# Weight conversion spread over the score units, masks moved to GpSimd, and products two blocks later, in a routed-attention and ELU kernel

## The chip, the cores and the metric

The kernel runs on one core of a Trainium2 chip. The metric is the device time of one execution in microseconds. Three runs of the kernel before took 1084.14, 1084.19 and 1082.23 us (median 1084.14). Its profile is of another execution, which took 1081.5 us with a span of 1078.2 us. The engines are called PE (matmuls; PEld is its weight load), DVE (VectorE), ACT (ScalarE), POOL (GpSimd) and SP (which issues the DMAs).

## The reference

Four batches of eight heads, 768 tokens of 64 elements each. Every query and key is assigned to one of 16 centroids of its head; attention is allowed only where the two assignments agree. Its output, as 3072 tokens of 512, goes through an MLP with an ELU.

```python
mask = q_assign[:, :, :, None] == k_assign[:, :, None, :]
scores = scale * np.matmul(q, k.transpose(0, 1, 3, 2))
scores = np.where(mask, scores, -1000000000.0)
...
attn = np.exp(scores)
attn = attn / (np.sum(attn, axis=-1, keepdims=True) + 1e-09)
...
h = x @ w_in                       # 512 x 2048
g = np.where(h > 0.0, h, alpha * (np.exp(np.minimum(h, 0.0)) - 1.0))
return (g @ w_out).astype(np.float32)   # 2048 x 512
```

Both weights arrive as 64-bit floats, everything else as 32-bit.

## The kernel before, in words

**Blocks.** Attention is done in 48 blocks: four batches, three thirds of the queries (256 tokens), four pairs of heads. In a block, `scores(n)` has three units. A unit is 128x1024 scores in one PSUM buffer of two banks (matmuls L398 for q times k, L407 for the mask), which ACT turns into `p` with an exponential (L415). `values(n)` multiplies `p` with v into `o_bank` (L442) and sums the rows into a buffer `d` with a matrix of ones (L431): 24 matmul records from `p` itself or, where `sums(n)` has added the three units on DVE first (L419 to L421), only 4. ACT copies `o_bank` to `xT` (L456) and `d` to `r` (L458), DVE takes the reciprocal (L459), POOL multiplies (L460). `check(n)` reads `r` again on ACT for a running sum (L466). The units, `d` and the hidden matmuls share three PSUM buffers (`banks`).

**Masks.** `assign` makes one-hot assignments `hot` on DVE (L349 to L364) from similarities that PE computes (L332). `masks(n)` turns those of the queries into 0 or minus 2^80 (L375: m times x minus m, two instructions on ACT, 64x256 bf16 each) for the matmul L407 of block n.

**MLP.** After four blocks a third of the tokens is complete. Its MLP has four groups of work, one for each later block: hidden 0 and 1; hidden 2 and 3; products 1 to 4; products 5 to 7. `hidden` runs 32 matmuls (64 records, L481, for two of them), an exponential on ACT (L491), a clamp on POOL (L492) and `elu` on DVE (L498 to L502), which is issued one `hidden` late, from a list called `lag`. The product with `w_out` is done with seven half-size block products instead of eight (L511), in the manner of Strassen and Winograd: g is cut in four (a_, b_, c_, d_), `w_out` in four (e_, f_, g_, h_), and sums of the cuts are made once for the weights (`sum_weights`, on POOL and DVE, L296 to L299) and per third for g. The products alternate between the PSUM banks `o_bank` and `f_bank`.

**Weights.** The 64-bit weights are loaded as 32 pieces of 128x512 (16 of `w_in`, 16 of `w_out`), as pairs of 32-bit words, into memory that is free at the time. `weight_steps` is a generator; each step issues, for one piece: on DVE the mantissa bits (L252) and the exponent bits into a tile `ex` (L255); one step later, on ACT the mantissa to a float, 2^-20 x + 1 (L247), and the exponent's new bias (L248); on DVE the sign (L258) and the low word (L261); on POOL the final product (L264). `weigh(k)` takes k steps. It is called four times a step in blocks 0 to 3 and five after each step of the MLP in blocks 4 and 5; in block 6 what is left and `sum_weights` come before the first products.

**Order.** The order of work on each engine is that of the program's text. The main loop takes block n: `values(n-1)`, loads, `scores(n)`, `check(n-1)`, `masks(n+1)`, `sums(n)` from n = 6 on, then group n-4 of the MLP (`LAG = 4`). At the last block of a batch the next batch's routing (`similar`, `assign`) is spread between the steps of that group; with LAG at 4 this is the group of products 5 to 7.

Of the kernel before, what the change touches and what calls it, by code (L numbers as in the profile page):

```python
# [9 lines left out]
F32 = mybir.dt.float32  # L10
BF16 = mybir.dt.bfloat16
# [7 lines left out]
P = 128  # L19
# [41 lines left out]
def main_path(ctx, tc, c, q, k, v, centroids, moe_w_in, moe_w_out, out):  # L61
# [100 lines left out]
    for e in range(2):  # L162
# [4 lines left out]
            axis=Axis.XY,  # L167
            op=Alu.add,
        )
    minus = const.tile([P, 2], F32, name="minus")  # L170
    nc.vector.tensor_scalar(minus, big, -BIG, None, op0=Alu.mult)
    nc.vector.tensor_scalar(big, big, BIG, None, op0=Alu.mult)

    sq = const.tile([P, D], F32, name="sq")
# [37 lines left out]
    ]  # L212
    into = len(pieces)
    pieces += [(w_out[:, f], moe_w_out[ts(f, P)]) for f in range(FC)]
    one = const.tile([P, 1], F32, name="one")
    off = const.tile([P, 1], F32, name="off")
    nc.gpsimd.memset(one, 1.0)
    nc.gpsimd.memset(off, -896.0 * 2**23)
    words, exps = {}, {}
    places = []  # L220
# [19 lines left out]

    def weight_steps():

        for n in range(len(pieces) + 1) if wide else ():
            if n > 0:
                to = pieces[n - 1][0]
                ex = exps[n - 1]
                nc.scalar.activation(to, to.bitcast(U32), Act.Identity, scale=2.0**-20, bias=one)  # L247
                nc.scalar.activation(ex, ex, Act.Relu, scale=8.0, bias=off)  # L248
            if n < len(pieces):
                high = words[n][0][:, :, 1]  # L250
                e = exps[n] = loads.tile([P, WC], U32, name="ex", tag="ex", bufs=2)
                nc.vector.tensor_scalar(  # L252
                    pieces[n][0].bitcast(U32), high, 0xFFFFF, None, op0=Alu.bitwise_and
                )
                nc.vector.tensor_scalar(e, high, 0x7FF00000, None, op0=Alu.bitwise_and)  # L255
            if n > 0:
                w, place, limit = words.pop(n - 1)
                nc.vector.scalar_tensor_tensor(  # L258
                    ex, w[:, :, 1], 0x80000000, ex, op0=Alu.bitwise_and, op1=Alu.bitwise_or
                )  # L260
                nc.vector.scalar_tensor_tensor(  # L261
                    to, w[:, :, 0], 2.0**-52, to, op0=Alu.mult, op1=Alu.add
                )
                nc.gpsimd.tensor_tensor(to, to, ex.bitcast(F32), op=Alu.mult)  # L264
                places.append((place, limit))
                ask()
            yield
# [4 lines left out]
    places += [(spare[:, ts(n, 2 * WC)], into + 2 * n - 1) for n in range(FC * DM // (2 * WC))]  # L272
    ask()
    rest = weight_steps()

# [93 lines left out]
    def masks(n):  # L369
        b, third, pr = blocks[n]  # L370
        qm[n] = route.tile([P, QS], BF16, name="qm", tag="qm", bufs=2)
        for e in range(2):
            rows = slice(64 * e, 64 * e + 64)
            m = big[rows, pr % 2 : pr % 2 + 1]
            nc.scalar.activation(  # L375
                qm[n][rows],
                hot[b, 0][rows, side(pr, e), ts(third, QS)],
                Act.Identity,
                scale=m,
                bias=minus[rows, pr % 2 : pr % 2 + 1],  # L380
            )

# [5 lines left out]
    def scores(n):  # L388
        b, third, pr = blocks[n]
        i = b * NPR + pr  # L390
        cols = ts(third, QS)
        for u in range(NT // 2):
            s = banks()
            for m in range(2):
                kt = 2 * u + m
                for e in range(2):
                    rows = slice(64 * e, 64 * e + 64)
                    nc.tensor.matmul(  # L398
                        s[:, e, ts(m, QS)],
                        lhsT=T[i, 1][rows, ts(kt, P)],  # L400
                        rhs=T[i, 0][rows, cols],
                        start=True,
                        stop=False,
                    )
                for e in range(2):
                    rows = slice(64 * e, 64 * e + 64)
                    nc.tensor.matmul(  # L407
                        s[:, e, ts(m, QS)],
                        lhsT=hot[b, 1][rows, side(pr, e), ts(kt, P)],
                        rhs=qm[n][rows],  # L410
                        start=False,
                        stop=True,
                    )
# [48 lines left out]

    def check(n):

        seen_r = work.tile([P, QS], BF16, name="seen_r", tag="seen_r", bufs=1)
        nc.scalar.activation(seen_r, rs.pop(n), Act.Copy, accum_out=r_sum[:, n : n + 1])  # L466


    lag = []
# [36 lines left out]
                op=Alu.subtract,  # L506
            )

    def product(to, left, right, more=False):
        for f in range(FC // 2):  # L510
            nc.tensor.matmul(  # L511
                to[:, :QS],
                lhsT=left[:, f],
                rhs=right[:, f],
                start=(f == 0 and not more),
                stop=(f == FC // 2 - 1),
                skip_group_check=more,
            )

    def outer(b, third):  # L520
# [5 lines left out]
        seen = {}  # L526

        def temp():
            return loads.tile([P, 2, QS], F32, name="part", tag="ex", bufs=2)

        def out_tile():
            return work.tile([P, DM], F32, name="o_sb", tag="o_sb")
# [83 lines left out]
    for n in range(len(blocks) + LAG):  # L616
# [7 lines left out]
                load("k", (b + 1) * NPR + pr)  # L624
        if n + 1 < len(blocks):
            load_v(n + 1)
        if n < len(blocks):
            scores(n)
        if 0 < n <= len(blocks):
            check(n - 1)  # L630
        if n < len(blocks):
            if at + 1 < NB:
                masks(n + 1)
            if n >= LAG + 2:
                sums(n)
            if ahead and at in turns:
                for j in range(2):
                    turn((b + 1) * NPR + turns[at], j)
# [15 lines left out]
        for m, step in enumerate(main):  # L654
# [279 lines left out]
```

## Time and profile before

| what | from the profile | us |
|---|---|---|
| span | page | 1078.2 |
| PE busy, 27.7 to 161.5 us | busy time by stretch | 94.7 of 133.8 |
| PE busy, 188.5 to 1053 us | busy time by stretch | 863.4 of 864.5 |
| PE waiting for ACT's copy to `r` (L458) at L398 | waits | 27.4, six times |
| DVE waiting for ACT's exponent (L248) at L258 | waits | 24.2, six times |
| DVE's L255 waiting for POOL's product (L264) | waits | 13.9 + 12.8 |
| conversion on ACT: L247, L248 | groups | 23.0, 22.9 |
| conversion on POOL: L264 | groups | 22.1 + 21.7 |
| masks on ACT: L375 | groups | 56.8 (96 of 0.59) |
| clamp on POOL: L492, 1024 elements | groups | 1.06 each |

The page cuts the span in 40 slices of 27 us and gives the busy share of each engine in tenths; PEclk is the clock that PE was granted. A timeline line has start, duration, engine, line of the kernel, operation, output, inputs with shapes, and in brackets the idle time just before with what ended it. The span falls in two stages: to about 189 us PE is often idle while the weights are converted and summed; after that it is busy without a gap until the last products.

### The profile page before, as it was taken

How to read it: one execution, taken by the hardware profiler on the slowest of the kernel's cores; microseconds unless marked ns; L12 is line 12 of the kernel's file. 1: busy time of each engine (PE TensorE's matmuls, PEld its weight loads, DVE VectorE, ACT ScalarE, POOL GpSimd, SP SyncE). 2: the span in 40 equal slices, each digit the busy share in tenths (PEclk: the TensorE clock that was granted, in tenths of full speed). 3: DMA queues.
4: the chain of work that ended last, by engine and by line, in shares of the span. 5: the costliest groups of instructions: out<-in, count | busy, mean ns of one | idle time of the engine just before them, and what ended most of it. 6: DMA issues, size and time to landing. Idle time of an engine off the chain costs nothing.

```text
span 1078.2 us, 14856 instructions
## 1 busy us (share of the span) xinstructions
PE 1012.6 (94%) x6323; PEld 782.4 (73%) x6323; DVE 500.1 (46%) x624; ACT 381.9 (35%) x651; POOL 163.9 (15%) x164
## 2 busy tenths in 40 slices
PE   6778477999999999999999999999999999999996
PEld 4446355787688788787678788788678788788785
DVE  5565667444744334344744344344753344334231
ACT  4765451432333333432333333432243333432210
POOL 0333345110011111110011111110011111111110
PEclk9989688999999999999999999999999999999999
DMA  9734330131100230131100230131100100100000
GB/s 283 255 104 134 81 64 1 50 62 27 49 16 15 64 60 15 49 62 27 50 16 15 63 61 15 49 60 30 49 15 16 49 15 16 49 16 16 20 1 22
DMA packets 103960, 55.58 MB, mean 52 GB/s; under 512 B 83408, under 2 KB 96720, under 8 KB 103888
## 3 DMA queue, kind: packets, MB, share of 16 engines
q1 hardware_dynamic: 103888, 54.57, 18.8%
q8 instruction: 51, 0.84, 0.3%
q14 instruction: 21, 0.17, 0.0%
HBM read 48.27 MB, written 6.29 MB: 51 GB/s over the span
## 4 chain that ended last, share of the span: by engine, by line
PE 82%; DVE 9%; POOL 4%; issue 2%; ACT 2%; DMA 0%; POOLq 0%; ACTq 0%
PE banks L481 30%; PE f_bank L511 15%; PE o_bank L511 12%; PE banks L398 11%; PE o_bank L442 10%; PE banks L407 3%; PE banks L431 2%; POOL w_out L264 2%; POOL w_in L264 1%; DVE ex L258 1%; DVE oh L351 1%; PE banks L332 1%; DVE hot L361 1%; DVE ex L255 1%; DVE w_in L261 1%
## 5 line engine op out<-in xcount | busy, mean ns | idle before, releaser
L481 PE MATMUL banks<-xT,w_in 128*128 128x256 f32 x1536 | 338.4, 381 | 1.3 <-DVE gT L498 1.3
L481 PEld LDWEIGHTS banks<-xT,w_in 128*128 128x128 f32 x1536 | 290.5, 190 | 47.8 <-ACT p L415 3.2
L398 PE MATMUL banks<-qT,kT 64*128 64x256 f32 x1152 | 176.7, 404 | 38.1 <-ACT r L458 27.4
L415 ACT ACTIVATE p<-banks 128x1024 f32<-128x1024 f32 x144 | 147.0, 1025 | 46.8 <-PE banks L407 42.4
L459 DVE RECIPROCAL r<-r 128x256 f32<-128x256 f32 x48 | 84.0, 1750 | 161.8 <-ACT r L458 161.7
L398 PEld LDWEIGHTS banks<-qT,kT 64*128 64x128 f32 x1152 | 91.6, 195 | 90.2 <-ACT r L458 30.3
L442 PE MATMUL o_bank<-p,v_raw 128*64 128x256 f32 x1152 | 141.4, 386 | 0.0
L491 ACT ACTIVATE gT<-banks 128x1024 f32<-128x1024 f32 x48 | 49.1, 1023 | 240.9 <-PE banks L481 240.9
L498 DVE SCALAR_TENSOR_TENSOR gT<-gT,banks 128x1024 f32<-128x1024 f32 x48 | 58.4, 1216 | 163.0 <-POOL gT L492 163.0
L442 PEld LDWEIGHTS o_bank<-p,v_raw 128*64 128x64 f32 x1152 | 78.8, 137 | 51.7 <-issue 15.0
L492 POOL TENSOR_SCALAR gT<-gT 128x1024 f32<-128x1024 f32 x48 | 50.9, 1060 | 317.1 <-ACT gT L491 317.1
L511 PE MATMUL f_bank<-w_out,gT 128*128 128x256 f32 x384 | 89.8, 387 | 7.9 <-POOL w_out L297 7.9
L460 POOL TENSOR_TENSOR xT<-xT,r 128x256 f32<-128x256 f32 x48 | 38.6, 804 | 345.3 <-DVE r L459 345.3
L511 PE MATMUL o_bank<-w_out,gT 128*128 128x256 f32 x384 | 89.1, 386 | 0.0
L511 PEld LDWEIGHTS f_bank<-w_out,gT 128*128 128x128 f32 x384 | 73.8, 193 | 21.0 <-POOL w_out L297 9.0
L407 PE MATMUL banks<-qm,hot 64*128 64x256 bf16 x576 | 83.8, 277 | 2.8 <-DVE hot L361 2.8
L511 PEld LDWEIGHTS o_bank<-w_out,gT 128*128 128x128 f32 x384 | 73.1, 193 | 13.3 <-issue 3.5
L456 ACT COPY xT<-o_bank 128x256 f32<-128x256 f32 x48 | 17.8, 370 | 160.7 <-PE o_bank L442 160.7
L375 ACT ACTIVATE qm<-hot,minus,big 64x256 bf16<-64x256 bf16 x96 | 56.8, 591 | 35.4 <-DVE hot L361 34.2
L419 DVE TENSOR_TENSOR psum<-p 128x1024 f32<-128x1024 f32 x42 | 51.2, 1219 | 34.8 <-ACT p L415 34.8
L420 DVE TENSOR_TENSOR psum<-psum,p 128x1024 f32<-128x1024 f32 x42 | 52.8, 1257 | 4.9 <-ACT p L415 1.6
L511 PE MATMUL f_bank<-w_sum,g_sum 128*128 128x256 f32 x192 | 44.6, 386 | 0.5 <-ACT part L559 0.5
(110 smaller groups left out, 811.7 us busy)
## 6 DMA issues: line engine op xcount, KB each, us to landing
v_raw<-in_v_dram SPq DMA_DIRECT2D x48, 384.0 KB, 3.2
out_dram<-o_sb SPq DMA_DIRECT2D x24, 256.0 KB, 2.1
w_sum<-in_moe_w_out_dram SPq DMA_DIRECT2D x11, 512.0 KB, 3.7
q_raw<-in_q_dram SPq DMA_DIRECT2D x48, 96.0 KB, 3.9
k_raw<-in_k_dram SPq DMA_DIRECT2D x48, 96.0 KB, 3.4
w_sum<-in_moe_w_in_dram SPq DMA_DIRECT2D x8, 512.0 KB, 7.7
w_out<-in_moe_w_in_dram SPq DMA_DIRECT2D x8, 512.0 KB, 10.2
w_out<-in_moe_w_out_dram SPq DMA_DIRECT2D x5, 512.0 KB, 3.7
```

Of the source, the lines that this page charges most:

```text
L375: nc.scalar.activation(qm[n][rows], hot[b, 0][rows, side(pr, e), ts(third, QS)], Act.Identity, scale=m, bias=minus[rows, pr % 2 : pr % 2 + 1],
L398: nc.tensor.matmul(s[:, e, ts(m, QS)], lhsT=T[i, 1][rows, ts(kt, P)], rhs=T[i, 0][rows, cols], start=True, stop=False,)
L407: nc.tensor.matmul(s[:, e, ts(m, QS)], lhsT=hot[b, 1][rows, side(pr, e), ts(kt, P)], rhs=qm[n][rows], start=False, stop=True,)
L415: nc.scalar.activation(p, s, Act.Exp, scale=SCALE)
L419: nc.vector.tensor_tensor(to, pu[n, 0], pu[n, 1], op=Alu.add)
L420: nc.vector.tensor_tensor(to, to, pu[n, 2], op=Alu.add)
L442: nc.tensor.matmul(o_bank[64 * e : 64 * e + 64, :QS], lhsT=raw["v", n][:, e, kt], rhs=p[:, e, ts(m, QS)], start=(kt == 0), stop=(kt == NT ...
L459: nc.vector.reciprocal(r, r)
L481: nc.tensor.matmul(hf[:, f], lhsT=w_in[:, ch, ts(4 * n + f, P)], rhs=xT[b, third][:, ch], start=(ch == 0 and f % 2 == 0), stop=(ch == KC - 1),
L492: nc.gpsimd.tensor_scalar(t, t, 1.0, 0.0, op0=Alu.min, op1=Alu.max)
L498: nc.vector.scalar_tensor_tensor(t, t, -1.0, hf, op0=Alu.add, op1=Alu.max)
L511: nc.tensor.matmul(to[:, :QS], lhsT=left[:, f], rhs=right[:, f], start=(f == 0 and not more), stop=(f == FC // 2 - 1), skip_group_check=more,)
```

## The change

- `weight_steps` works over three pieces: in step k DVE does the two mantissa and exponent operations of piece k, ACT the exponent of piece k-1, and POOL the mantissa to float of piece k-1 (a `tensor_scalar` from uint32, which was ACT's L247), then DVE the sign and low word of piece k-2 and POOL the product of piece k-2. `ex` has three buffers instead of two.
- One step is issued after each of the three score units in blocks 0 to 7, and two after each step of the MLP in blocks 6 and 7. The four steps at the end of a block are gone.
- `LAG` is 6: each MLP group comes two blocks later, `sums` start at block 8, and the group beside the routing at a batch's end is now hidden 2 and 3.
- `masks` is a `tensor_scalar` on POOL, and is issued ahead of `scores(n)`. `minus` and `one` are gone.
- The second and third product change places and banks, and no product accumulates on another's bank; two ACT copies become DVE additions that read `f_bank`.
- `check` writes over `r`, and `sq` uses the buffer of `r`.

```diff
     def weight_steps():
-        for n in range(len(pieces) + 1) if wide else ():
-            if n > 0:
-                to = pieces[n - 1][0]
-                ex = exps[n - 1]
-                nc.scalar.activation(to, to.bitcast(U32), Act.Identity, scale=2.0**-20, bias=one)
-                nc.scalar.activation(ex, ex, Act.Relu, scale=8.0, bias=off)
+        for n in range(len(pieces) + 2) if wide else ():
             if n < len(pieces):
                 high = words[n][0][:, :, 1]
-                e = exps[n] = loads.tile([P, WC], U32, name="ex", tag="ex", bufs=2)
+                e = exps[n] = loads.tile([P, WC], U32, name="ex", tag="ex", bufs=3)
...
-            if n > 0:
-                w, place, limit = words.pop(n - 1)
+            if 0 <= n - 1 < len(pieces):
+                to, ex = pieces[n - 1][0], exps[n - 1]
+                nc.scalar.activation(ex, ex, Act.Relu, scale=8.0, bias=off)
+                nc.gpsimd.tensor_scalar(
+                    to, to.bitcast(U32), 2.0**-20, 1.0, op0=Alu.mult, op1=Alu.add
+                )
+            if n > 1:
+                to, ex = pieces[n - 2][0], exps.pop(n - 2)
+                w, place, limit = words.pop(n - 2)
...
-            nc.scalar.activation(
+            nc.gpsimd.tensor_scalar(
                 qm[n][rows],
                 hot[b, 0][rows, side(pr, e), ts(third, QS)],
-                Act.Identity,
-                scale=m,
-                bias=minus[rows, pr % 2 : pr % 2 + 1],
-            )
+                m,
+                m,
+                op0=Alu.mult,
+                op1=Alu.subtract,
+            )
+    LAG = 6
...
             nc.scalar.activation(p, s, Act.Exp, scale=SCALE)
+            if n < LAG + 2:
+                weigh(1)
...
-        seen_r = work.tile([P, QS], BF16, name="seen_r", tag="seen_r", bufs=1)
-        nc.scalar.activation(seen_r, rs.pop(n), Act.Copy, accum_out=r_sum[:, n : n + 1])
+        r = rs.pop(n)
+        nc.scalar.activation(r, r, Act.Copy, accum_out=r_sum[:, n : n + 1])
...
         def second():
-            product(f_bank, c_, f_)
-            nc.scalar.copy(seen["ae"][:, 1], f_bank[:, :QS])
+            product(f_bank, b_, g_)
+            o0, _ = seen["o"] = out_tile(), out_tile()
+            nc.vector.tensor_tensor(o0[:, :QS], f_bank[:, :QS], seen["ae"][:, 0], op=Alu.add)
+            nc.vector.tensor_tensor(b_, b_, g_sum, op=Alu.subtract)

         def third_():
-            product(o_bank, b_, g_, more=True)
-            seen["o"] = out_tile(), out_tile()
-            nc.scalar.copy(seen["o"][0][:, :QS], o_bank[:, :QS])
-            nc.vector.tensor_tensor(b_, b_, g_sum, op=Alu.subtract)
+            product(o_bank, c_, f_)
+            nc.scalar.copy(seen["ae"][:, 1], o_bank[:, :QS])

         def fourth():
-            product(f_bank, d_, t4, more=True)
+            product(f_bank, d_, t4)
             seen["dt"] = temp()
-            nc.scalar.copy(seen["dt"][:, 0], f_bank[:, :QS])
+            nc.vector.tensor_tensor(
+                seen["dt"][:, 0], f_bank[:, :QS], seen["ae"][:, 1], op=Alu.add
+            )
...
-    LAG = 4
...
+        if n + 1 < len(blocks) and at + 1 < NB:
+            masks(n + 1)
         if n < len(blocks):
             scores(n)
         if 0 < n <= len(blocks):
             check(n - 1)
         if n < len(blocks):
-            if at + 1 < NB:
-                masks(n + 1)
...
-        if n < LAG:
-            weigh(4)
...
             if n < LAG + 2:
-                weigh(5)
+                weigh(2)
```

The conversion's lines in the changed kernel are L244 and L247 (mantissa and exponent bits, DVE), L250 (exponent, ACT), L251 (mantissa to float, POOL), L257 and L260 (sign, low word, DVE) and L263 (product, POOL). L374 is the masks, L401 and L410 the score matmuls, L464 the reciprocal, L465 the `xT` product, L548 and L553 the first two DVE operations of the products.

More of the change, by code (lines that the diff above doesn't have):

```diff
@@ L169, in main_path @@
         )
-    minus = const.tile([P, 2], F32, name="minus")
-    nc.vector.tensor_scalar(minus, big, -BIG, None, op0=Alu.mult)
     nc.vector.tensor_scalar(big, big, BIG, None, op0=Alu.mult)
-    sq = const.tile([P, D], F32, name="sq")
+    sq = work.tile([P, D], F32, name="sq", tag="r", bufs=1)
     ss = const.tile([P, 1], F32, name="ss")
@@ L214, in main_path @@
     pieces += [(w_out[:, f], moe_w_out[ts(f, P)]) for f in range(FC)]
-    one = const.tile([P, 1], F32, name="one")
     off = const.tile([P, 1], F32, name="off")
-    nc.gpsimd.memset(one, 1.0)
     nc.gpsimd.memset(off, -896.0 * 2**23)
@@ L271, in main_path @@
     spare = w_out.rearrange("p f m -> p (f m)")
-    places += [(spare[:, ts(n, 2 * WC)], into + 2 * n - 1) for n in range(FC * DM // (2 * WC))]
+    places += [(spare[:, ts(n, 2 * WC)], into + 2 * n - 2) for n in range(FC * DM // (2 * WC))]
     ask()
@@ L507, in elu, with product @@
             )
-    def product(to, left, right, more=False):
+    def product(to, left, right):
         for f in range(FC // 2):
@@ L514, in product @@
                 rhs=right[:, f],
-                start=(f == 0 and not more),
+                start=(f == 0),
                 stop=(f == FC // 2 - 1),
-                skip_group_check=more,
             )
@@ L528, in temp @@
         def temp():
-            return loads.tile([P, 2, QS], F32, name="part", tag="ex", bufs=2)
+            return loads.tile([P, 2, QS], F32, name="part", tag="ex", bufs=3)
         def out_tile():
```

## The prediction

> **What bounds the kernel now.** I read the page's slices first: PE is at 9 tenths from the eighth slice (189 us) on and far below it before, so there are two stages.
>
> ```profile
> span 1078.2 us, 14856 instructions
> PE   6778477999999999999999999999999999999996
> DVE  5565667444744334344744344344753344334231
> POOL 0333345110011111110011111110011111111110
> PEclk9989688999999999999999999999999999999999
> ```
>
> Busy time by stretch says the same: PE is busy 863.4 of the 864.5 us from 188.5 on, but 94.7 of 133.8 between 27.7 and 161.5 us, where the 32 weight pieces are converted. Only two things can move the span: that first stage, and new holes in PE's later work. The timeline of DVE and of POOL shows what paces the conversion:
>
> ```profile
> 35.37 0.43 DVE L255 TENSOR_SCALAR ex<-w_sum 128x512 uint32<-128x512 uint32 x1 [1.16 <-POOL w_in L264]
> 35.72 0.68 DVE L258 SCALAR_TENSOR_TENSOR ex<-w_sum,ex 128x512 uint32<-128x512 uint32 x1
> 36.32 0.69 DVE L261 SCALAR_TENSOR_TENSOR w_in<-w_sum,w_in 128x512 f32<-128x512 uint32 x1
> 36.92 0.42 DVE L252 TENSOR_SCALAR w_in<-w_sum 128x512 uint32<-128x512 uint32 x1
> 37.08 1.39 POOL L264 TENSOR_TENSOR w_in<-w_in,ex 128x512 f32<-128x512 f32 x1 [1.74 <-DVE w_in L261]
> 38.50 0.43 DVE L255 TENSOR_SCALAR ex<-w_sum 128x512 uint32<-128x512 uint32 x1 [1.16 <-POOL w_in L264]
> ```
>
> One piece takes 38.50 - 35.37 = 3.13 us and is a closed ring: L255 waits until POOL's product L264 has freed the `ex` buffer, then L258, L261, and the next L264. Once per block a piece takes 6.0 us (L264 starts at 40.22, then at 46.22), since ACT waits for the reciprocal and does the masks (1.2 us) ahead of it. Four pieces and a block take 15.4 us (reciprocals at 40.05, 55.43, 70.82). The last L264 ends at 161.5, and two sum passes follow. The fourth product ends at 188.5, where the next values begin: that instant is my marker.
>
> The second thing to see is how DVE and POOL meet:
>
> ```profile
> 109.85 1.27 POOL L264 TENSOR_TENSOR w_out<-w_out,ex 128x512 f32<-128x512 f32 x1 [1.74 <-DMA w_sum<-in_moe_w_out_dram]
> 111.09 1.47 POOL L492 TENSOR_SCALAR gT<-gT 128x1024 f32<-128x1024 f32 x1
> 111.59 1.26 DVE L252 TENSOR_SCALAR w_out<-w_out 128x512 uint32<-128x512 uint32 x1
> 166.47 2.72 DVE L421 TENSOR_TENSOR psum<-psum 128x512 f32<-128x512 f32 x1
> ```
>
> L252 takes 0.42 elsewhere and here ends 0.29 after POOL's L492 does; L421 takes 0.69 elsewhere and here outlasts a POOL subtraction. They exclude each other.
>
> **What the skill says.** The Trainium skill, "SBUF — State Buffer", section "Who interferes with whom": GpSimd shares a port pair with DVE's two-port operations (tensor_scalar) and with those that read two SBUF tensors, the second one blocks fully, others do not contend. The four lines agree, and the reciprocal (1.75 us, beside L264's 1.27 at 40.22) is indeed untouched. "GPSIMD Engine Reference", section "3.1 Elementwise — side-by-side cycle accounting": a body of up to two operations costs 1.03 cycles an element (at 1.2 GHz, section "1. Specifications"). The trace's L492 at 1024 elements takes 1.04 us uncontended, so 0.88 + 0.16 fixed.
>
> **The change part by part.**
>
> *The ring.* With three `ex` buffers L247 (L255 before) waits for the product of piece k-3, but products now lag two steps, so this is again the product issued just before it on POOL. The ring is not shortened. It is lengthened: between that product and the next, POOL now holds the new L251 (multiply and add, 512 elements from uint32), next in its queue and ready. It shuts out DVE's L247, L257 and L260 while it runs. Estimate for L251: 0.44 + 0.16 = 0.60 us. No POOL operation on uint32 is in the trace: 0.50 if it is cheaper than L492's rate, 1.38 if it costs what L264 does; I take 0.60. A blocked DVE operation loses less than the full wait (after 112.56 the next began 0.20 later, not the usual 0.35), so the ring is 3.13 + 0.60 - 0.15 = 3.58 us. ACT's removed Identity (32 x 0.72 = 23 us) was not in the ring; it leaves only ACT's waits, below.
>
> *A block of three pieces.* From the end of one L260: the reciprocal holds DVE 1.6 us, beside the last product; then `xT` by `r` on POOL (0.8), two masks on POOL, L251 and DVE's four operations alternate. Masks (64x256): 0.22 + 0.16 = about 0.4 each by the rule above; 0.3 to 0.7 as bounds (ACT's are 0.59). The first piece ends at 1.6 + 0.8 + 0.8 + 1.4 = 4.6, the second 4.0 later (its product and L251 cannot hide in the reciprocal), the third 3.6: 12.2 us. PE needs 5.3 (values) + 3.3 (scores) = 8.6 and ACT 3 x (1.03 + 0.72) + 1.6 = 6.9, so DVE and POOL set it. ACT no longer has masks and Identity before the Relu, so 6.0 for the piece at the reciprocal does not recur.
>
> *The sum to the last product.* The first reciprocal, after PE's values(0) (28.8 + 5.3, begun 0.4 earlier because ACT has no masks before the kT copies), starts at 34.8. Six blocks of 12.2 (n = 1 to 6): 108.1. Four pieces beside hidden 0 and 1, with two clamps (1.05) and elu 0 (1.8): 16.7, so 124.8. Block 7: 137.0. Six pieces with two clamps and elu 1 to 3, of which the first-operand passes hide beside products: 24.7, so the last product ends at 161.7, against 161.5 before. Eight instead of six blocks of scores and values are done by then. PE (28 us of hidden matmuls after 96) is not the bound in it.
>
> *The sum stage.* Before: reciprocal at 161.95, fourth product's end 26.6 later. After: reciprocal at 160.4. The masks on POOL (0.8) and L421's collision nearly cancel. Products 1 and 2 need no summed weights now (b_ and g_ instead of c_ and f_) and lie beside the sums; but the fourth writes f_bank, and its reader L553 stands on DVE behind both sums and L548 (1.22), so the whole fourth (3.45) comes after that. DVE's last sum ends 18.8 after the reciprocal (179.2), + 1.22 + 0.42 = 180.9, + 3.45 and gaps: 185.2. Gain at the marker 188.5 - 185.2 = 3.3.
>
> *Work already done at the marker.* Two blocks more: each 6.63 (205.77 to 212.40 in the chain). 13.3. Their row sums from unsummed p (24 instead of 4 matmuls each) lie in the first stage, hidden.
>
> *Later.* PE-bound, nothing gained. ACT's masks (2 x 0.59 a block) and the copies that became DVE reads are hidden under PE. But at the three batch changes hidden 2 and 3, not products 5 to 7, now stand beside the routing. Before, the last product (3.45) lay between the k similarity and the new scores:
>
> ```profile
> 294.93 0.57 PE L407 MATMUL banks<-qm,hot 64*128 64x256 bf16 x2 [0.27 <-DVE hot L361]
> ```
>
> After, the k similarity is PE's last work. DVE has elu 3 (waits for exp and clamp, until 4.2 us after hidden 3 ends), then two halves of assign (2.6 and 2.3, ready for scores at 6.8 and 9.3), while PE arrives at 5.2. Stall 1.5 + 0.6 = 2.1; less 0.3 as before, 1.8 x 3 = 5.6 us lost. The tail, six groups instead of four, stays dense; product 2 waits 0.2 for elu 3.
>
> *Free edits.* In-place check, `sq` in r's buffer, the dropped `minus` and `one` (0.17 and 0.10): startup or behind ACT's exponentials, nothing. DMA order: pieces are asked at least six ahead of use (3.7 us to land).
>
> Sum: 3.3 + 13.3 - 5.6 - 0.2 = 10.8, so the profiled span goes from 1078.2 to 1067. That execution took 1081.5 us; the runs 1082.2 to 1084.2, median 1084.1. The forecast is 1084.1 - 10.8 = 1073.3.
>
> **The rivals.**
> *B, the collisions do not happen.* L251 and the masks fit beside DVE. Ring 3.13 over some 30 pieces gains 13, the masks 6 more: 1054. For it: L258 lasts 0.68 in many places where POOL starts. Against: the four lines above.
> *C, slower: GpSimd's step from uint32 is slow.* At 1.2 us it adds 30 x 0.6 = 18: 1091. It decides from 0.60 + 10.8/30 = 0.96 us on. For it: L264 takes 1.38 for as many elements. Against: it has two inputs, L492's one-input rate is half of that.
> *D, no change.* L251 at 0.8 (-6) and masks at 0.7 (16 x 0.3 = -5) eat it: the new work in the shared stage is worth what the dropped ACT waits were. 1084.
>
> **How the numbers follow.** A 0.50, own range 1066 to 1080; B 0.17; C 0.20; D 0.13. What a measurement can tell from no change is 0.2%, 2.2 us. Faster is A, B and some of D, 0.71; same 0.06; slower C and the rest of D, 0.23. The range 1056 to 1091 leaves out part of B and the far end of C.
>
> **What would show it.** Right: L251 near 0.6 us; L247 near 1.0 instead of 0.43, blocked behind L251; L257 starts 3.5 to 3.6 apart within a block; reciprocals 12.2 apart for n = 1 to 5; the last L263 ends near 162 and the fourth product near 185, held by L553; three stalls near 2 us of L410 on `hot`. Wrong: L251 over 1 us (C), or L247 still 0.43 and blocks near 10 us (B), or PE waits outside the batch changes after 190 us.

## The result, and the profile after

Four runs of the changed kernel took 1075.99 to 1077.86 us, median 1077.78; the kernel before had a median of 1083.18. The ratio is 0.9949, with a 95% interval of 0.9929 to 0.9969: faster by 5.4 us, where 10.8 were forecast. The two profiled executions differ by less, 1078.2 against 1076.1 us of span, since the one of before took 1081.5 us, the low end of its runs, and the one of after 1077.86, the high end. Stage by stage I compare these two spans: 2.1 us gained, where the sum said 10.8. So 8.7 us of the sum went wrong, and that is larger than the miss of the total time shows.

The page after, head and slices of 27 us, and the group of the masks (busy time, mean ns of one):

```profile
span 1076.1 us, 14909 instructions
PE   7868785899999999999999999999999999999997
DVE  5666677548425425538524425538534424424131
POOL 2677778222322223122322222222322222221010
...
L374 POOL TENSOR_SCALAR qm<-hot,big 64x256 bf16<-64x256 bf16 x96 | 145.6, 1516 | 21.5 <-DVE hot L360 16.7
```

POOL, which had 5 tenths at most in the first stage, has 6 to 8 in six of its first seven slices now. The masks are its largest group over the whole span, 145.6 us, 1.52 us each where the forecast had 0.4. PE stands at 9 tenths one slice later than before.

One block of the conversion, from reciprocal to reciprocal, on DVE (start, duration, then in brackets the idle time before it and what ended it):

```profile
48.25 0.69 DVE L260 SCALAR_TENSOR_TENSOR w_in<-w_sum,w_in 128x512 f32<-128x512 uint32 x1
48.86 1.74 DVE L464 RECIPROCAL r<-r 128x256 f32<-128x256 f32 x1
50.52 0.36 DVE L244 TENSOR_SCALAR w_in<-w_out 128x512 uint32<-128x512 uint32 x1
50.80 0.94 DVE L247 TENSOR_SCALAR ex<-w_out 128x512 uint32<-128x512 uint32 x1
51.66 0.68 DVE L257 SCALAR_TENSOR_TENSOR ex<-w_sum,ex 128x512 uint32<-128x512 uint32 x1
52.26 0.68 DVE L260 SCALAR_TENSOR_TENSOR w_in<-w_sum,w_in 128x512 f32<-128x512 uint32 x1
52.87 0.61 DVE L244 TENSOR_SCALAR w_in<-w_out 128x512 uint32<-128x512 uint32 x1
57.28 0.43 DVE L247 TENSOR_SCALAR ex<-w_out 128x512 uint32<-128x512 uint32 x1 [3.81 <-POOL w_in L263]
57.62 1.10 DVE L257 SCALAR_TENSOR_TENSOR ex<-w_sum,ex 128x512 uint32<-128x512 uint32 x1
58.65 0.68 DVE L260 SCALAR_TENSOR_TENSOR w_in<-w_sum,w_in 128x512 f32<-128x512 uint32 x1
...
60.83 0.43 DVE L247 TENSOR_SCALAR ex<-w_out 128x512 uint32<-128x512 uint32 x1 [1.17 <-POOL w_in L263]
...
62.19 0.68 DVE L260 SCALAR_TENSOR_TENSOR w_in<-w_out,w_in 128x512 f32<-128x512 uint32 x1
62.79 1.74 DVE L464 RECIPROCAL r<-r 128x256 f32<-128x256 f32 x1
```

and on POOL in the same time (x2 is both masks of a block):

```profile
50.68 0.78 POOL L465 TENSOR_TENSOR xT<-xT,r 128x256 f32<-128x256 f32 x1 [0.38 <-DVE r L464]
51.45 3.74 POOL L374 TENSOR_SCALAR qm<-hot,big 64x256 bf16<-64x256 bf16 x2
55.28 0.62 POOL L251 TENSOR_SCALAR w_in<-w_in 128x512 f32<-128x512 uint32 x1
55.98 1.27 POOL L263 TENSOR_TENSOR w_in<-w_in,ex 128x512 f32<-128x512 f32 x1
57.34 0.85 POOL L251 TENSOR_SCALAR w_in<-w_in 128x512 f32<-128x512 uint32 x1
```

Three things are to be seen. The ring of one piece, from L247 to the next L247, is 60.83 - 57.28 = 3.55 us (3.58 forecast). The new L251 takes 0.62 alone (0.60 forecast), and a DVE instruction that meets it is lengthened: L257, 1.10 instead of 0.68. But DVE stands idle for 3.81 us in the middle of the block, for a product L263 that is queued on POOL behind both masks and L251. The block takes 62.79 - 48.86 = 13.93 us, where 12.2 were forecast.

The sum stage (PE's own lines, then three of POOL and DVE in it) and one batch change after:

```profile
184.74 3.78 PE L516 MATMUL o_bank<-w_out,gT 128*128 128x256 f32 x8 [5.79 <-POOL w_out L296]
191.48 3.28 PE L516 MATMUL o_bank<-w_out,gT 128*128 128x256 f32 x8 [2.95 <-POOL w_out L296]
194.55 4.06 PE L516 MATMUL f_bank<-w_sum,gT 128*128 128x256 f32 x16
...
175.31 3.50 POOL L374 TENSOR_SCALAR qm<-hot,big 64x256 bf16<-64x256 bf16 x2
178.89 2.34 POOL L295 TENSOR_TENSOR w_sum<-w_out 128x1024 f32<-128x1024 f32 x1
193.56 0.41 DVE L553 TENSOR_TENSOR o_sb<-f_bank,part 128x256 f32<-128x256 f32 x1
...
265.05 0.57 PE L410 MATMUL banks<-qm,hot 64*128 64x256 bf16 x2 [0.66 <-DVE hot L360]
...
267.41 0.57 PE L410 MATMUL banks<-qm,hot 64*128 64x256 bf16 x2 [0.27 <-DVE hot L360]
```

The fourth product starts where the third one ends; it is the third that waits, twice, for POOL's difference L296. On POOL both masks of a block stand ahead of the weight sums, which begin with L295. The fourth product's end, the marker, is at 198.5. The batch change costs two waits of 0.66 and 0.27 us, each of them three times.

### The profile page after: what moved, and what is told of

Its sections match the earlier page's. It is cut to its first block, busy times and chain, and to the rows that moved or that the text cites. A ratio compares the mean times of both kernels' runs of the same rounds, so it can differ in the third digit from the quotient of the medians.

```text
span 1076.1 us, 14909 instructions
## 1 busy us (share of the span) xinstructions
PE 1014.5 (94%) x6363; PEld 785.1 (73%) x6363; DVE 523.3 (49%) x641; ACT 292.8 (27%) x499; POOL 332.2 (31%) x291
## 4 chain that ended last, share of the span: by engine, by line
PE 78%; DVE 10%; POOL 8%; issue 3%; ACT 0%; DMA 0%; POOLq 0%; DVEq 0%
PE banks L486 27%; PE f_bank L516 15%; PE o_bank L516 11%; PE banks L401 10%; PE o_bank L447 10%; POOL qm L374 3%; PE banks L410 3%; DVE ex L257 2%; PE banks L436 2%; DVE r L464 1%; POOL w_in L263 1%; POOL w_out L263 1%; DVE ex L247 1%; DVE w_out L260 1%; DVE gT L503 1%
## 5 line engine op out<-in xcount | busy, mean ns | idle before, releaser
L401 PE MATMUL banks<-qT,kT 64*128 64x256 f32 x1152 | 175.8, 403 | 22.7 <-DVE gT L503 15.4
L374 POOL TENSOR_SCALAR qm<-hot,big 64x256 bf16<-64x256 bf16 x96 | 145.6, 1516 | 21.5 <-DVE hot L360 16.7
L464 DVE RECIPROCAL r<-r 128x256 f32<-128x256 f32 x48 | 84.0, 1750 | 133.7 <-ACT r L463 133.6
L401 PEld LDWEIGHTS banks<-qT,kT 64*128 64x128 f32 x1152 | 91.3, 194 | 75.0 <-DVE gT L503 16.7
L465 POOL TENSOR_TENSOR xT<-xT,r 128x256 f32<-128x256 f32 x48 | 38.5, 801 | 274.6 <-DVE r L464 274.6
L516 PE MATMUL o_bank<-w_out,gT 128*128 128x256 f32 x384 | 91.4, 392 | 8.8 <-POOL w_out L296 8.7
L410 PE MATMUL banks<-qm,hot 64*128 64x256 bf16 x576 | 83.6, 276 | 4.5 <-DVE hot L360 4.4
L516 PE MATMUL f_bank<-w_out,gT 128*128 128x256 f32 x384 | 86.8, 379 | 0.0
L425 DVE TENSOR_TENSOR psum<-psum,p 128x1024 f32<-128x1024 f32 x40 | 55.5, 1387 | 4.4 <-ACT p L418 0.6
## 6 DMA issues: line engine op xcount, KB each, us to landing
w_out<-in_moe_w_in_dram SPq DMA_DIRECT2D x8, 512.0 KB, 10.4
```

Source lines behind the costliest of these rows:

```text
L374: nc.gpsimd.tensor_scalar(qm[n][rows], hot[b, 0][rows, side(pr, e), ts(third, QS)], m, m, op0=Alu.mult, op1=Alu.subtract,)
L401: nc.tensor.matmul(s[:, e, ts(m, QS)], lhsT=T[i, 1][rows, ts(kt, P)], rhs=T[i, 0][rows, cols], start=True, stop=False,)
L410: nc.tensor.matmul(s[:, e, ts(m, QS)], lhsT=hot[b, 1][rows, side(pr, e), ts(kt, P)], rhs=qm[n][rows], start=False, stop=True,)
L425: nc.vector.tensor_tensor(to, to, pu[n, 2], op=Alu.add)
L464: nc.vector.reciprocal(r, r)
L516: nc.tensor.matmul(to[:, :QS], lhsT=left[:, f], rhs=right[:, f], start=(f == 0), stop=(f == FC // 2 - 1),)
```

## The experiments

Theory M: the masks on GpSimd are what the sum had too cheap; they stand in POOL's queue ahead of the piece that DVE waits for. Rivals: R, the mantissa step L251 is (its 0.62 us, and the exclusion, that is, DVE's wait while GpSimd is in its instruction); B, the number of `ex` buffers is (DVE's L247 waits for a buffer that a fourth one would spare it); P, the order of the products and the sum stage. All edits below are to the changed kernel. In the profile of every version with products six blocks later, the time from the marker to the end is 877.4 to 878.0 us: what these edits win or lose lies before the marker.

### The masks back on ACT

```diff
-            nc.gpsimd.tensor_scalar(qm[n][rows], hot..., m, m, op0=Alu.mult, op1=Alu.subtract)
+            nc.scalar.activation(qm[n][rows], hot..., Act.Identity, scale=m, bias=minus...)
...
-            masks(n + 1)
             scores(n)
             check(n - 1)
+            masks(n + 1)
```

> The changed kernel with one part undone: the masks are again two ACT instructions after check, everything else as changed. Theory M (the masks are what the forecast mis-sized: on POOL one takes 1.2 us alone and 1.9 inside the conversion, not 0.4, and stands between two products of the ring): a block falls from 13.9 to about 11.6 us, eight blocks give 18 us, the fourth product ends near 179 instead of 198.5, and the time is about 1058. Rival R (the ring with POOL's mantissa step sets the blocks and the masks lie beside it): blocks stay above 13 us and the time stays within 3 us of 1077.8. Later than the fourth product nothing should change in either theory, since PE is busy there.

Measured: 1058.79 us (1058.03 to 1059.78), ratio to the kernel before 0.9772 [0.9758, 0.9786]. DVE's side of a block:

```profile
47.25 1.74 DVE L465 RECIPROCAL r<-r 128x256 f32<-128x256 f32 x1
...
53.25 0.43 DVE L249 TENSOR_SCALAR ex<-w_out 128x512 uint32<-128x512 uint32 x1 [1.16 <-POOL w_in L265]
53.59 1.10 DVE L259 SCALAR_TENSOR_TENSOR ex<-w_sum,ex 128x512 uint32<-128x512 uint32 x1
...
58.75 1.74 DVE L465 RECIPROCAL r<-r 128x256 f32<-128x256 f32 x1
```

The wait of 3.81 has become one of 1.16, and the block is 58.75 - 47.25 = 11.5 us. The marker is at 180.3 instead of 198.5. 19.0 us come back from one edit that touches the masks alone. M holds: with the masks where they were, the rest of the change is worth 24 us. The edit moves the masks to another engine and behind `scores` and `check`; no run separates the two.

### The mantissa step back on ACT

```diff
-                nc.gpsimd.tensor_scalar(to, to.bitcast(U32), 2.0**-20, 1.0, op0=Alu.mult, op1=Alu.add)
+                nc.scalar.activation(to, to.bitcast(U32), Act.Identity, scale=2.0**-20, bias=one)
```

> The changed kernel with the mantissa step (L251 on POOL) back on ACT as an Identity, masks left on POOL. Theory R (POOL's step lengthens the ring by 0.42 us a piece): L257 starts 3.13 apart again within a block, 30 pieces give 12 us, time about 1065. Rival M (masks hold the blocks): each block still has 3.7 us of masks between products, and only the two of three pieces that do not stand beside the masks get shorter; 5 to 8 us, time 1070 to 1073. Against both: ACT, in order, is late with the exponent behind its exponentials, DVE waits for it as in the kernel before, and the time stays at 1076 to 1080.

Measured: 1062.53 us (1061.77 to 1063.3), ratio 0.9812 [0.9797, 0.9826]; a ring of 3.13 and blocks of 12.4 us, the masks still 3.75 us a pair. It gained 15.3 us, more than either theory had put on it. L251 costs 1.5 us a block (three times the 0.42 by which the ring falls, and some). R is right that this step costs much; but the forecast had this cost (3.58 against 3.13), so it isn't what the forecast missed. And ACT, which gets 32 instructions of 0.72 us back, did not hold up DVE's conversion: its list of waits has no wait of a conversion step for ACT.

### A fourth exponent buffer

```diff
-                e = exps[n] = loads.tile([P, WC], U32, name="ex", tag="ex", bufs=3)
+                if n % 4 < 3:
+                    e = loads.tile([P, WC], U32, name="ex", tag="ex", bufs=3)
+                else:
+                    e = work.tile([P, 2, 2 * QS], F32, name="psum", tag="psum", bufs=1)
...
```

> The changed kernel with a fourth exponent buffer (the sum tile, idle until block 8), so that DVE's exponent extraction no longer waits for the product issued just before it. Theory P (DVE's operations on two SBUF tensors or in two-port form and POOL's exclude each other, so the ring is their sum 0.35 + 0.35 + 0.60 + 0.60 + 0.62 + 1.3 = 3.8 whatever the buffers are): L257 starts stay 3.4 to 3.8 apart, blocks 13.5 to 14, time within 3 us of 1077.8. Theory B (the wait for the buffer is the ring): DVE needs 2.0 a piece and POOL 1.9, so a block falls towards 3 x 2.0 + 1.7 + part of the masks, about 10 us, and the time to about 1050.

Measured: 1069.81 us (1068.99 to 1070.74), ratio 0.9879 [0.9865, 0.9894]: between the two theories. DVE's block now:

```profile
51.89 0.72 DVE L262 SCALAR_TENSOR_TENSOR ex<-w_sum,ex 128x512 uint32<-128x512 uint32 x1
54.45 0.69 DVE L265 SCALAR_TENSOR_TENSOR w_in<-w_sum,w_in 128x512 f32<-128x512 uint32 x1 [1.84 <-POOL w_in L256]
55.05 1.50 DVE L249 TENSOR_SCALAR w_in<-w_out 128x512 uint32<-128x512 uint32 x1
56.47 0.83 DVE L252 TENSOR_SCALAR ex<-w_out 128x512 uint32<-128x512 uint32 x1
57.23 1.76 DVE L262 SCALAR_TENSOR_TENSOR ex<-w_out,ex 128x512 uint32<-128x512 uint32 x1
```

No L252 (the step that fills the new buffer) waits for a product any more. What was a wait is now spread over instructions that are blocked while they run: 1.50 for 0.42, 1.76 for 0.68, and one wait for POOL's mantissa. The block fell by 1.1 us only, to 12.9. The wait for the third buffer is thus for the smaller part a matter of buffers. The larger part, as these lines read, is POOL's work in that time, which DVE meets wherever it goes on.

### The second and third product in the old order

```diff
         def second():
-            product(f_bank, b_, g_)
+            product(f_bank, c_, f_)
...
         def third_():
-            product(o_bank, c_, f_)
+            product(o_bank, b_, g_)
```

> The changed kernel with products 2 and 3 in their old order and banks (c_ f_ on f_bank second, b_ g_ on o_bank third; the two DVE reads stay). In the changed kernel the second product lies beside the weight sums. If that is worth a product, products 3 and 4 both follow the last weight sum and the fourth product ends 3 us later, 201.5 instead of 198.5; time 1081. If the DVE read of f_bank behind the sums gives it back, the time does not move.

Measured: 1080.08 us (1079.19 to 1081.82), ratio 0.9977 [0.9968, 0.9987]; the fourth product ends at 200.9 instead of 198.5. The new order is worth 2.3 us and not a loss, so P is not the cause of the miss.

### Both back on ACT, and then no GpSimd at all

```diff
-                nc.gpsimd.tensor_tensor(to, to, ex.bitcast(F32), op=Alu.mult)
+                nc.vector.tensor_tensor(to, to, ex.bitcast(F32), op=Alu.mult)
```

The first kernel has both edits to ACT above, the second this one besides.

> The masks and the mantissa step both back on ACT, everything else as changed. Theory S (each GpSimd step costs the shared ring its own time, so the two losses add): masks alone gave back 19.0 us and the mantissa step alone 15.3, together 34, so 1043 to 1047; the ring is 3.1 us and a block of three pieces near 10. Theory A (ACT takes over as the pacer: exponentials 3 x 1.03, mantissa and exponent 6 x 0.72, masks 1.2 and copies 1.6 make 10.2 us a block in order, and DVE's sign step waits for ACT's exponent again): only a few us below the better of the two alone, 1053 to 1059, with waits of DVE on ACT of over 1 us a block.

Measured: 1045.61 us (1045.22 to 1047.14), ratio 0.9654 [0.9636, 0.9672], with reciprocals 10.3 us apart. The two losses nearly add: 19.0 + 15.3 = 34.3 would give 1043.5. That ACT would pace it instead is refuted, although ACT is busy 9.2 us of each block.

> As both_act, and the final product of each piece is on DVE instead of GpSimd, so that the conversion uses no GpSimd instruction at all. Theory X (what limits a piece is the exclusion of GpSimd's product and DVE): DVE alone needs 0.35 + 0.35 + 0.6 + 0.6 + 0.65 = 2.55 us a piece, three pieces and a reciprocal of 1.6 are 9.3 us a block against PE's 8.6, so blocks near 9.5 us and 1033 to 1041. Theory A (ACT paces, 10.2 us a block): no gain over both_act, within 3 us of it.

Measured: 1042.03 us (1042.00 to 1042.66), ratio 0.9619 [0.9603, 0.9635]: only 3.6 us more, a little outside both expectations. Reciprocals are 9.96 us apart, not 9.5. A part of it can be read in the timeline of DVE (this is the last experiment below, where the block is the same): L251 meets POOL's `xT` by `r` and is lengthened from 0.42 to 0.95.

### The masks with constants

```diff
-                m,
-                m,
+                1.0,
+                1.0,
                 op0=Alu.mult,
                 op1=Alu.subtract,
```

> The masks stay on GpSimd, with the constants 1.0 and 1.0 in place of the two operands that are read for each partition; so the masking of the scores is left out (0 or -1 is added to them instead of 0 or -2^80). Theory O (the two per-partition operands are what makes GpSimd's mask slow): a mask falls from 1.2 (shortest in the changed kernel) to near 0.4 us, and the time to about 1060. Theory T (the bf16 tile or GpSimd's fixed cost is slow): the mask stays above 1.1 us and the time within 3 us of 1077.8.

Measured: 1069.95 us (1069.32 to 1070.69), ratio 0.9875 [0.9858, 0.9893]. The shortest mask falls from 1.21 to 1.06 us and a pair in the conversion from 3.74 to 2.64. Neither theory: the operands per partition cost 0.15 us alone, but something else makes up nearly all of the 1.2. A pair fell by 1.10, though, where two masks at 0.15 less give 0.30. The lines of one block show the rest:

```profile
62.16 1.23 POOL L374 TENSOR_SCALAR qm<-hot 64x256 bf16<-64x256 bf16 x1
62.39 0.88 DVE L257 SCALAR_TENSOR_TENSOR ex<-w_out,ex 128x512 uint32<-128x512 uint32 x1
```

The first mask runs almost freely here and L257 waits (0.88 for 0.68). In the changed kernel L257 ran in its 0.68 and the first mask took 2.42. So by these lines most of this gain came from who went first: the block is 12.81 us with the subtraction still in it. Why that changed is not shown.

### The mask's form by itself

Two kernels with extra instructions on a scratch tile, each eight times, in blocks where GpSimd is mostly idle. Of each only the durations are read.

> The changed kernel with seven extra instructions on GpSimd on a scratch tile of 64x256 elements, eight times, in blocks where GpSimd is idle most of the time; only the fastest of each is to be read. They are: bf16 to bf16 with two operands per partition (the mask's form); the same with two constants; with one constant and one operation; bf16 to f32, f32 to bf16 and f32 to f32 with two constants; f32 to f32 with two operands per partition. Theory D (bf16 is what makes the mask slow): 1.0 to 1.2 us for the bf16 forms and 0.4 us for f32 to f32, whether with constants or not. Theory F (a fixed price of the per-partition or of the small shape): f32 to f32 is above 0.8 us too. Theory O (number of operations): the form with one operation is near half of that with two.

> The changed kernel with eight extra GpSimd instructions on a scratch tile, eight times, to find what in the mask's form costs 1.2 us where the clamp of 128x1024 takes 1.04: 64x256 f32 with multiply and add; 64x256 f32 with min and max (the clamp's operations); 64x256, 64x512, 128x512 and 128x256 f32 with multiply and subtract; 128x256 with multiply and add; 64x256 bf16 with two operands per partition, multiply and add. Theory U (the subtraction is slow): multiply and add, and min and max, near 0.4 us at 64x256, multiply and subtract above 1 us in all shapes, and twice as long at 512 elements as at 256. Theory W (64 partitions are slow): 128x256 with multiply and subtract near 0.4 us, and 64x256 above 1 us whatever the operations.

The answers by line (min/median/max in ns; then first and last start, and the shape). From the first kernel: the mask's form, the same with constants, and one multiplication alone, all in bf16.

```profile
L673 POOL TENSOR_SCALAR part<-part,big x8: 1212/1213/1214, 322.0 to 888.0; 64x256 bf16<-64x256 bf16 x8
L674 POOL TENSOR_SCALAR part<-part x8: 1062/1062/1062, 323.3 to 889.3; 64x256 bf16<-64x256 bf16 x8
L675 POOL TENSOR_SCALAR part<-part x8: 848/849/851, 324.5 to 890.5; 64x256 bf16<-64x256 bf16 x8
L678 POOL TENSOR_SCALAR part<-part x8: 1301/1302/1306, 328.2 to 894.2; 64x256 f32<-64x256 f32 x8
```

L673 repeats the mask's 1.21 exactly, so this is the price of the instruction and not of its place. L678 is the same in f32 with constants: 1.30, no cheaper, so bf16 is not it. From the second kernel, all f32 with constants: multiply and add; min and max; then multiply and subtract in two shapes; then 128x256, subtract and add.

```profile
L674 POOL TENSOR_SCALAR part<-part x8: 398/399/399, 323.3 to 889.3; 64x256 f32<-64x256 f32 x8
L675 POOL TENSOR_SCALAR part<-part x8: 392/393/393, 323.8 to 889.8; 64x256 f32<-64x256 f32 x8
L676 POOL TENSOR_SCALAR part<-part x8: 1062/1062/1062, 324.3 to 890.3; 64x256 f32<-64x256 f32 x8
L677 POOL TENSOR_SCALAR part<-part x8: 1915/1916/1917, 325.4 to 891.4; 64x512 f32<-64x512 f32 x8
L679 POOL TENSOR_SCALAR part<-part x8: 1328/1337/1339, 330.3 to 896.3; 128x256 f32<-128x256 f32 x8
L680 POOL TENSOR_SCALAR part<-part x8: 404/404/405, 331.7 to 897.7; 128x256 f32<-128x256 f32 x8
```

Theory U holds: 0.40 with an addition, which is the 0.4 of the forecast, and 1.06 to 1.34 with a subtraction, on 64 and on 128 partitions. (L676 and L677 write in place; to another tile, as L678 of the first kernel does, 64x256 took 1.30, about as long as the 1.34 for 128x256.) From 256 to 512 elements the subtraction grows by 0.85 us, 3.3 ns an element, where the clamp's 1.04 us for 1024 elements is at most 1.0 ns. The operands per partition cost 0.15 in bf16, but in f32 the first kernel's form with them took 1.21, less than the 1.30 with constants. That one multiplication in bf16 (0.85) is dearer than two operations in f32 (0.40) fits no theory here, and is left open.

### The masks as m times x plus (-m)

```diff
+    minus = const.tile([P, 2], F32, name="minus")
+    nc.vector.tensor_scalar(minus, big, -BIG, None, op0=Alu.mult)
...
                 m,
-                m,
+                minus[rows, pr % 2 : pr % 2 + 1],
                 op0=Alu.mult,
-                op1=Alu.subtract,
+                op1=Alu.add,
```

> The masks stay on GpSimd where the change put them, but as m times x plus (-m) instead of m times x minus m, with -m kept in a small tile as in the kernel before: the same values. Theory U (the subtraction is what GpSimd is slow at): a mask falls from 1.2 us alone to 0.55 to 0.86, a pair in the conversion from 3.74 to 1.3 to 1.9 us, a block from 13.93 to about 12.0, and the time to 1062 to 1066. Theory V (what is slow is the bf16 tile with operands per partition): a mask stays at 1.2 us and the time within 3 us of 1077.8.

Measured: 1066.74 us (1066.46 to 1068.03), ratio 0.9854 [0.9838, 0.9871]. One mask alone, then a pair in the conversion and its first mask; last the first mask of the changed kernel's pair:

```profile
210.91 0.55 POOL L376 TENSOR_SCALAR qm<-hot,big,minus 64x256 bf16<-64x256 bf16 x1
...
61.80 2.46 POOL L376 TENSOR_SCALAR qm<-hot,big,minus 64x256 bf16<-64x256 bf16 x2
61.80 1.75 POOL L376 TENSOR_SCALAR qm<-hot,big,minus 64x256 bf16<-64x256 bf16 x1
...
51.45 2.42 POOL L374 TENSOR_SCALAR qm<-hot,big 64x256 bf16<-64x256 bf16 x1
```

With the same values and the same place, addition in place of subtraction was worth 11.0 us, a little less than expected. Alone a mask takes 0.55; the pair in the conversion takes 2.46 and not the 1.3 to 1.9 expected, and the block is 12.66 us. The first of the two is 1.2 us longer there than alone, and in the changed kernel its 2.42 is also 1.2 more than 1.21. In the block of the changed kernel above, DVE still runs L247, L257 and L260 until 52.94 when the first mask has begun at 51.45. So the 1.2 us is by all signs the exclusion, the same in both kernels, and the rest was the operation.

### Other distances of the products

```diff
-    LAG = 6
+    LAG = 4
```

> The changed kernel with the products four blocks behind again: a piece beside each unit in blocks 0 to 5, two after each MLP step in blocks 4 and 5, weights summed in block 6. Theory L (the prediction's: two more blocks done by the marker are worth 13.3 us, less 2.5 for the stalls at the batch changes): the first stage loses two blocks of 13.9 us and gains six pieces of about 3.9 us at the MLP steps, 4 us less; in all +13.3 - 4 - 2.5 = +7, 1083 to 1086. Theory N (the later products are worth nothing, because blocks of 13.9 us replace what PE would do in 6.6): within 3 us of 1077.8 or below, and the four waits of L410 over 0.5 us at each batch change are gone.

Measured: 1084.00 us (1082.77 to 1085.83), ratio 1.0007 [1.0000, 1.0014]. So without the two later blocks the change gains nothing. The fourth product ends at 191.1, 7.4 earlier than with six, and from there to the end of the span it is 892.0 us instead of 877.6: 14.4 longer. The waits for `hot` at the batch changes are gone, but PE waits for a mask on POOL six times instead, 3.9 us in all. Theory L gave the time, but both its parts were some 3.5 us too small (4 for the 7.4, 10.8 for the 14.4) and cancelled. N is refuted.

The best version takes both lessons: no GpSimd in the conversion, and seven blocks.

> The conversion without GpSimd (masks and mantissa on ACT, final product on DVE), and the products seven blocks behind instead of six. Theory L (work done in the first stage is worth its full PE time later): one more block of scores and values is done by the end of the fourth product, worth 6.6 us; the first stage gains a block of 10.0 us and loses three pieces of 2.6 us at the MLP steps, 2.2 us longer: 4.4 less than with six, 1037 to 1039. Rival E (the later work or its buffers take it back, for example at the batch changes, where other groups now stand beside the routing): 1041 to 1044, with new waits of PE after 190 us.

Measured: 1034.91 us (1033.22 to 1035.30), ratio 0.9563 [0.9548, 0.9579], 7.1 us below the same with six. That is more than the 4.4 expected. In the two profiles (9.0 us apart, since this one is the fastest of its four runs) the marker is 3.8 later, and the time after it 12.8 shorter: PE is busy 9.9 less there, and the waits for `hot` (2.8 us in all with six) are absent. Its chain between 30 and 140 us:

```profile
by line: DVE ex L259 16.9%; DVE ex L251 12.7%; DVE r L465 12.2%; DVE w_in L265 9.4%; DVE w_out L262 8.9%; DVE w_in L262 8.4%; DVE w_out L265 8.3%; DVE w_out L248 5.5%; DVE w_in L248 3.7%; DVE gT L504 3.2%; issue 3.0%; PE banks L437 2.0%; PE
```

and the place in a block that keeps it from the 9.3 us a block of the expectation for the conversion without GpSimd:

```profile
54.64 1.75 DVE L465 RECIPROCAL r<-r 128x256 f32<-128x256 f32 x1
...
56.59 0.95 DVE L251 TENSOR_SCALAR ex<-w_out 128x512 uint32<-128x512 uint32 x1
```

The chain of the first stage is nearly all DVE now, which is busy 112.0 us of 116.3 between 27.7 and 144.0. PE is busy 111.6 in that time, so a faster DVE would soon meet it.

## Why the prediction was right, and which of its sizes were not

1077.8 us lies in the range given and in the own range of the likeliest case (1066 to 1080), at half of the gain forecast. Its mechanism held in part. Of its signs, L251 near 0.6 and the distance of 3.5 to 3.6 came, this only between the second and third piece of a block; L247 at 1.0, blocks of 12.2, the last product near 162, the fourth product near 185 behind L553 and stalls near 2 us did not. Two errors of opposite sign stand behind the figure, and one of them is large. That they partly cancelled is luck.

**The ring: right.** Forecast 3.58, measured 3.55, by the mechanism named, with one detail turned round: L247 was to be the blocked instruction at 1.0 us. It stays at 0.43, since DVE is first when the product ends; L257 then meets L251 and is blocked, 1.10. The sum is the same.

**The masks: the term that was too small.** "Two masks on POOL ... about 0.4 each by the rule above; 0.3 to 0.7 as bounds." They take 1.21 alone, outside the bounds. The rule was the Trainium skill's ("GPSIMD Engine Reference", "3.1 Elementwise — side-by-side cycle accounting": a body of up to two operations costs 1.03 cycles an element), checked against L492 of the trace, whose operations are min and max. The runs confirm it for min and max (0.39) and for multiply and add (0.40), and contradict it for multiply and subtract (1.06 to 1.34). I priced the mask by a line that agreed in engine, instruction and number of operations, but not in the operations themselves.

**A block of three pieces: 12.2 forecast, 13.93 measured.** With the addition it is 12.66, so 1.27 of the 1.73 us come back with another operation. The other 0.46 are not separated: the masks' own price is still 0.3 above the sum's (two of 0.55), and the exclusion adds 1.2 to the first. The sum also had the order wrong. It put the masks before DVE's four operations, with the pieces ending 4.6, 8.6 and 12.2 after the last L260 of the block before; in the trace L260 ends 4.0, 10.4 and 13.9 after it (48.94). DVE goes first, so the first piece is not late at all, and the second, which waits for the first one's product behind the masks, takes the whole loss.

**To the last product: 161.7 forecast, 173.3 measured.** Seven blocks of 1.73 are 12.1, and 161.7 + 12.1 = 173.8. Everything else in this sum held: the first reciprocal at 34.91 (34.8), the block with hidden 0 and 1 at 30.4 = 13.9 + 16.5 (16.7), the one with hidden 2 and 3 at 36.9.

**The sum stage: 24.8 forecast, 26.6 measured.** "The fourth ... held by L553" failed: the third product is held, by POOL's L296, and the fourth follows without a gap. L553 ends at 193.97, only 0.6 before that, so the two paths are nearly equal. The miss of 1.8 us is for the most part the masks again: 3.50 us on POOL ahead of the weight sums, where the sum had 0.8. With the masks on ACT the stage takes 24.5 us (reciprocal at 155.76, next values at 180.26), with the addition 25.4. With 11.5 at the reciprocal it makes the marker 13.3 late, 198.5 for 185.2. Against the kernel before the stage gains nothing (26.6 there too), but undoing the new order costs 2.3, so the order about made up for what the masks cost here.

**Work already done: 13.3 forecast.** PE's busy time after the marker fell from 880.2 to 865.5 us, 14.7; and with four blocks of delay the time after the marker is 14.4 longer. The step holds, and is a little larger.

**The batch changes: 5.6 forecast, 2.0 measured.** PE waits 0.66 + 0.27 us for `hot` at each of three changes, 2.8 in all, against 0.8 before. The first half is ready 5.9 us after hidden 3 ends instead of 6.8, and the copy of the second half was not an extra wait. PE's idle time after the marker rose by 2.6 us in all (9.5 to 12.1). So the later stage gained 14.7 - 2.6 = 12.1, not the 7.5 of the sum; this hid 4.6 of the 13.3 lost at the marker, and 8.7 remained.

**The prediction's rivals.** C put a loss on GpSimd's step from uint32, at 1.2 us; that step cost 0.62, as forecast. What C said of that step was true of the masks beside it, so its mechanism was right at the wrong instruction. D named the masks, at 0.7 us each: the right term, still too small; its other term, L251 at 0.8, was not the miss. B, no collisions, is refuted by the lines above: L257 at 1.10 for 0.68, a mask at 2.42 for 1.21.

## What to carry to other kernels

When work moves to another engine, look for a line with the same operation there, not only the same instruction and number of operations; where there is none, keep a bound wide enough for a slow operation, and measure it by itself first (0.40 against 1.06 us here). Where GpSimd and DVE share one ring, work on GpSimd can hold DVE as well: in a block here the three mantissa steps (0.62 each alone) cost 1.5 us, and the pair of masks, 3.74 on POOL, cost 2.4. The same conversion with less of GpSimd went from 1077.8 to 1045.6 us, and with none of it and one block more of delay to 1034.9. Look at a less busy engine too: ACT took both steps back, and no run shows a wait of the conversion for it. PE waited for a mask on ACT, 1.1 to 5.2 us in all, but only before the marker, where PE is not the limit.

## What the runs showed of the hardware

GpSimd's multiply and subtract costs 1.06 (in place) to 1.30 us for 64x256 and 1.34 for 128x256 in f32, multiply and add 0.40 for both. Two operands per partition add 0.15 in bf16. The exclusion of DVE and GpSimd (the Trainium skill, "SBUF — State Buffer", "Who interferes with whom": the one that issues second fully blocks) shows on GpSimd's side as well: a mask of 0.55 or 1.21 alone took 1.75 or 2.42 beside DVE's operations. Which one is second can't be read from the start in the record: the mask at 51.45 was kept out by L257 and L260, which begin after it and still took 0.68 each, while the mask with constants made L257 wait. With a fourth buffer the waits reappeared inside the instructions, 1.50 and 1.76 us for 0.42 and 0.68. A wait that vanishes from the list of waits may so have become a longer busy time.
